# Four more modelled steps in the start-up order of a conv and ELU kernel, with a smaller ScalarE copy, an earlier change of the conv's place and a longer modelled turn

## The chip, the cores and the metric

The kernel runs on one core of one Trainium2 chip. The metric is the device time of one execution in microseconds (us), as the median of several.

## The reference, cut to what matters

```python
# x (8, 4096, 192); weight (8, 7); w_in (192, 2048); w_out (2048, 192)
w = softmax(weight, axis=-1)                 # per head, 7 taps
att = causal depthwise conv of x with w      # 8 heads of 24 channels
h = att.reshape(32768, 192) @ w_in
g = where(h > 0, h, exp(min(h, 0)) - 1)      # ELU
out = g @ w_out
```

Of the kernel before, what the change touches and what calls it, by code (L numbers as in the profile page):

```python
# [34 lines left out]
O_AT = (12, 16)  # L35
CONV_AT = (14, 18, 22, 26)
CONV_POS = ((4, 4), (4, 4), (4, 4), (4, 4))
POS_FROM = 30
QB = 2
WARM = (6, 1, 4)  # L40
WCOLS = ((0, 4 * FC), (4 * FC, 16 * FC))
# [13 lines left out]
HELD = {"h": 2900.0, "c": 1300.0, "a": 1400.0}  # L55

EARLY_CONV = (7, 8, 9, 10)
LATE_Q, COPY_AT = 10, 6
LIVE, UNTIL = 16, 16
EARLY_O = (4, 8)  # L60
LANDS = {"x": {1: 7200.0, 2: 14200.0}, "w_in": 10200.0, "w_out": (3900.0, 8400.0, 11000.0)}
DONE_PE, TO_ACT, TO_POOL, TO_DVE, TO_PE = 165.0, 40.0, 85.0, 35.0, 60.0
ACT_H, ACT_C, ACT_O, POOL_H, DVE_H = 495.0, 470.0, 390.0, 578.0, 600.0
ENDS_ACT, ENDS_POOL, ENDS_DVE, TRANSPOSED = 103.0, 37.0, 84.0, 5000.0
TURNS = 260.0
X_AT = ((2, 1, 1), (1, 1, 0))
ZERO_AT = 8
TAIL = 18
# [2 lines left out]
def bass_lightweight_conv__then__act_elu_kernel(  # L71
# [95 lines left out]
    def o_items(k, g, rt, qs, visit, first, final):  # L167
# [4 lines left out]
        def issue(i):  # L172
# [8 lines left out]
            if ends:  # L181
                visits[k, g] = visit + 1
                turned[k, g] = clock[rt] + MM_O + TURNS

# [147 lines left out]
    for n in range(LIVE, NP):  # L332
# [5 lines left out]
        for m in conv_steps.get(n, []):  # L338
            for rt, later in enumerate(CONV_POS[m % CU] if n >= POS_FROM else (0, 0)):
                later += 3 * rt  # L340
# [770 lines left out]
```

## The kernel before: the parts that the change and the argument touch

The tokens are worked in 32 "supers" of 1024, and each super in 16 blocks of 128 hidden columns: 512 "steps". A step makes two "units", one for each group of 512 tokens. A unit is three H matmuls into one PSUM bank, exp on ScalarE, a clamp on GpSimd, and the ELU join on VectorE, which frees the bank. Sixteen output matmuls a step follow some steps later, and every fourth step has a conv tile, which also takes a bank for a while and is copied out by ScalarE (`csb`). The output accumulators hold two banks and are copied out by ScalarE too (`osb`). Each H or output matmul uses one half of the 128 partitions, so that two can run side by side; the halves are called row groups. The two row groups add to the same accumulator in turns: one waits until the other's visit has ended.

The order of TensorE is fixed when the program is built, by a small planner. It puts each item at a planned time and sorts. Up to step `LIVE` it picks whatever the model says is ready; up to step `UNTIL` it keeps a fixed list for each step but moves its clock on where the model says that something is not ready; after that it only adds up durations:

```python
LATE_Q, COPY_AT = 10, 6      # up to which block ScalarE copies w_in to the upper partitions
LIVE, UNTIL = 16, 16         # live picking, then modelled lists, up to these steps
TURNS = 260.0                # modelled gap between two visits of one accumulator
POS_FROM = 30                # from which step convs go inside the step
CONV_POS = ((4, 4), (4, 4), (4, 4), (4, 4))

def modelled():
    return step[0] < UNTIL

def take_bank(what, rt):                  # the bank that comes free first
    b = min(range(NBANK), key=lambda b: freed[b])
    if modelled():
        clock[rt] = max(clock[rt], freed[b])
    ...

def issue(i):                             # an output matmul
    take_bank(("a", k, g), rt)
    if modelled():
        clock[rt] = max(clock[rt], gt_at[t, g], turned.get((k, g), 0.0) if ... else 0.0)
    ...
for n in range(LIVE, NP):                 # steps after the live part
    ...
    for m in conv_steps.get(n, []):       # convs of super 2: steps 14, 18, 22, 26
        for rt, later in enumerate(CONV_POS[m % CU] if n >= POS_FROM else (0, 0)):
            later += 3 * rt
            lists[rt][later:later] = c_items(m, rt)
```

The upper half of the partitions needs its own copy of w_in. ScalarE and VectorE copy the first blocks, a DMA those from `LATE_Q` on:

```python
if i == COPY_AT:                                        # on ScalarE, after its unit 6
    W(s_w[1], 48)
    upper_half(UPPER[2][0], FC * LATE_Q)
...
c0, c1 = FC * LATE_Q, FF                                # on SyncE
sy.dma_start(w_in[HP:P, :, c0:c1], w_in[0:HP, :, c0:c1]).then_inc(s_wd, 16)
```

## Time and profile before

| What | Value |
|---|---|
| median of the first three runs | 720.21 us (720.03 to 720.96) |
| span of the profiled run | 718.9 us |
| TensorE busy | 99% of the span |
| first H matmul; first VectorE unit | 11.63 us; 14.33 us |
| step 16, 20, 24 (first H matmul) | 31.71, 36.95, 42.37 us |
| four steady steps | 5.44 us |
| last matmul ends | 714.88 us |

The step times are the starts of the first H matmul of a step, found by setting the trace's matmul records beside the program's own order (the counts agree). One more view belongs here, the waits between 31 and 43 us, so steps 16 to 24. It reads "who waited, for whom: us in total, times, longest"; PEld is TensorE's weight load, and in this view a matmul that waits at the head of the queue mostly shows as the wait of its weight load.

```profile
PEld H L1029 <- PE H L1029: 0.9, 4, 0.3
PEld H L1006 <- ACT csb L748: 0.5, 2, 0.3
PEld H L981 <- DVE gT L868: 0.5, 1, 0.5
ACT E L752 <- PE H L1006: 0.4, 1, 0.4
PEld H L1006 <- ACT osb L759: 0.4, 1, 0.4
PEld H L1006 <- DVE gT L868: 0.2, 1, 0.2
```

(Three lines of the view are left out.) The first line is output matmuls that wait for their turn on an accumulator. The second is H tiles whose bank was a conv's, the third the conv of step 18 (L981), which waits for VectorE to free its bank. The fourth is ScalarE, starved by it. The fifth is an H tile (L1006) of step 20, which was given the bank of an output accumulator and waits for ScalarE to copy that out.

### The profile page before, as it was taken

The page shows a single profiled execution, that of the slowest core. Times are in us where ns is not written, and L with a number is a line of the kernel's source. Part 1 is how long each engine was busy: PE and PEld are TensorE (multiplying, and loading weights), DVE is VectorE, ACT ScalarE, POOL GpSimd, SP SyncE. Part 2 cuts the span into 40 slices and gives each one's busy share as a digit, 9 for nine tenths or more (in the row PEclk, how much of TensorE's full clock was granted, in tenths as well). Part 3 has the DMA queues.
Part 4 walks back from the last instruction along what each step waited for, and adds up shares of the span by engine and source line. Part 5 has one row for each costly group of instructions (what it writes and reads, how often), then busy time and mean ns, then how long its engine had stood idle before and what let it go on. Part 6 is the DMA issues. An engine that isn't in the chain of part 4 may idle for free.

```text
span 718.9 us, 27610 instructions
## 1 busy us (share of the span) xinstructions
PE 712.0 (99%) x11847; PEld 683.3 (95%) x11847; DVE 641.5 (89%) x1048; ACT 678.5 (94%) x1289; POOL 664.4 (92%) x1112
## 2 busy tenths in 40 slices
PE   8999999999999999999999999999999999999997
PEld 4699999999999999999999999999999999999997
DVE  7999898998898998899998899988989988999993
ACT  6999999999999999999999999999999999999993
POOL 9989999999999999999999999999999999999893
PEclk9999999999999999999999999999999999999999
DMA  9725434554443553554553344554345544435312
GB/s 178 114 60 83 76 74 75 95 87 70 77 86 72 91 93 63 77 87 80 87 92 67 73 77 94 86 70 86 76 75 96 87 65 79 89 73 84 55 50 68
DMA packets 132303, 58.75 MB, mean 82 GB/s; under 512 B 98374, under 2 KB 131604, under 8 KB 132180
## 3 DMA queue, kind: packets, MB, share of 16 engines
q0 software_dynamic: 43504, 16.77, 22.5%
q1 hardware_dynamic: 88388, 39.32, 22.2%
q8 instruction: 93, 1.52, 0.9%
q10 hardware_dynamic: 288, 0.88, 0.4%
q14 instruction: 30, 0.25, 0.1%
HBM read 34.63 MB, written 25.46 MB: 84 GB/s over the span
## 4 chain that ended last, share of the span: by engine, by line
PE 95%; POOL 2%; DVE 1%; ACT 1%; issue 0%; DVEq 0%; POOLq 0%
PE H L1029 54%; PE H L1006 37%; PE H L981 4%; DVE gT L868 1%; POOL xg L622 1%; ACT E L752 1%; POOL w_in L642 0%; POOL w_out L653 0%; ACT csb L748 0%; POOL E L705 0%; POOL owner L670 0%; ACT osb L759 0%; DVE osb L859 0%; POOL block L680 0%; POOL ident L659 0%
## 5 line engine op out<-in xcount | busy, mean ns | idle before, releaser
L868 DVE SCALAR_TENSOR_TENSOR gT<-E,H 128x512 f16<-128x512 f32 x1024 | 632.0, 683 | 62.2 <-POOL E L705 58.3
L1006 PE MATMUL H<-att,w_in 64*128 64x512 bf16 x3072 | 680.8, 376 | 0.7 <-DVE gT L868 0.5
L1029 PE MATMUL H<-w_out,gT 64*128 64x192 f16 x8192 | 680.7, 243 | 0.1
L705 POOL TENSOR_SCALAR E<-E 128x512 f32<-128x512 f32 x1024 | 603.2, 612 | 41.5 <-ACT E L752 33.9
L1029 PEld LDWEIGHTS H<-w_out,gT 64*128 64x128 f16 x8192 | 608.5, 94 | 16.4 <-PE H L1029 1.6
L752 ACT ACTIVATE E<-H 128x512 f32<-128x512 f32 x1024 | 585.4, 601 | 24.0 <-PE H L1006 1.0
L1006 PEld LDWEIGHTS H<-att,w_in 64*128 64x128 bf16 x3072 | 274.3, 93 | 7.3 <-issue 1.4
L981 PE MATMUL H<-xg,Tm 64*128 64x240 bf16 x496 | 90.9, 263 | 0.2 <-DVE gT L868 0.2
L748 ACT ACTIVATE csb<-H 112x480 bf16<-112x480 f32 x124 | 70.8, 571 | 0.1
L759 ACT ACTIVATE osb<-H 128x384 f32<-128x384 f32 (+1 forms) x129 | 61.9, 482 | 6.9 <-PE H L1029 6.8
L622 POOL DMA_DIRECT2D xg<-in_x_dram x62 | 55.3, 896 | 0.2 <-issue 0.2
L981 PEld LDWEIGHTS H<-xg,Tm 64*128 64x128 bf16 x496 | 42.5, 94 | 1.2 <-DVE gT L868 0.5
L859 DVE COPY osb<-H 128x192 f32<-128x192 f32 x1 | 0.4, 358 | 7.3 <-PE H L1029 7.3
L903 PE MATMUL H<-zw 128*128 128x512 bf16 x10 | 4.0, 548 | 1.2 <-DVE zw L767 1.2
L727 ACT ACTIVATE xb<-xs 128x512 bf16<-128x512 f32 x3 | 1.7, 619 | 2.4 <-DMA xs<-in_x_dram 2.4
L957 PE MATMUL H<-xT,taps 128*128 128x256 bf16 (+1 forms) x24 | 3.9, 317 | 0.0
L903 PEld LDWEIGHTS H<-zw 128*128 128x128 bf16 x10 | 1.1, 125 | 2.8 <-issue 1.4
L957 PEld LDWEIGHTS H<-xT,taps 128*128 128x128 bf16 x24 | 2.2, 97 | 1.5
L642 POOL DMA_DIRECT2D w_in<-in_moe_w_in_dram x6 | 3.6, 610 | 0.0
L653 POOL DMA_DIRECT2D w_out<-in_moe_w_out_dram x3 | 2.5, 869 | 0.0
L720 ACT ACT_TABLE_LOAD x1 | 1.3, 1283 | 1.2 <-PEq L1096 1.2
L733 ACT ACTIVATE w_in<-w_in 64x1536 bf16<-64x1536 bf16 (+1 forms) x2 | 2.3, 1162 | 0.0
(43 smaller groups left out, 19.6 us busy)
## 6 DMA issues: line engine op xcount, KB each, us to landing
out_dram<-osb SPq DMA_DIRECT2D x126, 192.0 KB, 2.8
xg<-in_x_dram POOLq DMA_DIRECT2D x61, 240.0 KB, 4.6
xs<-in_x_dram ACTq DMA_DIRECT2D x1, 768.0 KB, 4.6
w_in<-in_moe_w_in_dram POOLq DMA_DIRECT2D x3, 192.0 KB, 5.4
att<-csb SPq DMA_TRANSPOSE x31, 3.8
w_out<-in_moe_w_out_dram POOLq DMA_DIRECT2D x2, 192.0 KB, 10.1
w_out<-in_moe_w_out_dram POOLq DMA_DIRECT2D x1, 384.0 KB, 13.2
conv_band<-wband SPq DMA_DIRECT2D x1, 288.0 KB, 7.0
```

The lines of the kernel that those rows point to most:

```text
L622: g.dma_start(xg[0:rows, b, 2 * w0 + gr : 2 * w1 : 2, :], src).then_inc(s_x[b][gr], 16)
L642: g.dma_start(w_in[0:HP, j, c0:c1], bass.AP(tensor=moe_w_in.tensor, offset=8 * j * FF + c0, ap=[[CPH * FF, HEADS], [FF, 8], [1, c1 - c0]], ...
L705: g.tensor_scalar(out=E[:, i % NE, :], in0=E[:, i % NE, :], scalar1=1.0, scalar2=0.0, op0=ALU.min, op1=ALU.max,).then_inc(s_clp)
L748: a.activation(*conv_evac(W, m), ACT.Copy).then_inc(s_ce)
L752: a.activation(E[:, i % NE, :], H[:, bank_of[item], :], ACT.Exp).then_inc(s_exp)
L759: a.activation(*out_evac(W, *item[1:]), ACT.Copy).then_inc(s_oev[item[2]])
L868: v.scalar_tensor_tensor(out=gT[:, s % NG3, q, u, :], in0=E[:, i % NE, :], scalar=1.0, in1=H[:, bank_of[item], :], op0=ALU.subtract, op1=A ...
L903: pe.matmul(H[:, bank, :], zw[:, 0:P], zw[:, 0:GS], start=True, stop=True)
L957: ins = pe.matmul(H[:, bank_of[item] + half, c0:c1], taps[:, tap, :], xT[:, j, HALO - PAD + tap + c0 : HALO - PAD + tap + c1], start=(tap ...
L981: ins = pe.matmul(H[:, bank_of["c", m], 256 * q : 256 * q + UC], Tm[rows, h, :], xg[rows, s % NXB, :, CPH * h : CPH * (h + 1)].rearrange(" ...
L1006: ins = pe.matmul(H[:, bank_of[item[:3]], :], w_in[HP * r : HP * (r + 1), j, FC * q : FC * (q + 1)], att[HP * r : HP * (r + 1), s % 2, j, ...
L1029: ins = pe.matmul(acc_of(k, g)[:, D * kb : D * (kb + 1)], gT[HP * rt : HP * (rt + 1), t % NG3, q, g, t0 : t0 + P], w_out[HP * rt : HP * (r ...
```

## The change

It aims at the start: the planner shall know of waits for four more steps, ScalarE shall copy half as much of w_in, the convs of steps 22 and 26 shall stand where those of later steps stand, and the turn of an accumulator shall be planned with more room.

```diff
-POS_FROM = 30
+POS_FROM = 19
...
-LATE_Q, COPY_AT = 10, 6
-LIVE, UNTIL = 16, 16
+LATE_Q, COPY_AT = 9, 6
+LIVE, UNTIL = 16, 20
...
-TURNS = 260.0
+TURNS = 320.0
```

## The prediction

> **What bounds the kernel now.** I read the page first, then two-microsecond and longer windows of the first 60 us, then the chain of waits there, then each engine's timeline there. A "step" below is one of the kernel's 512 blocks of 128 hidden columns for 1024 tokens; it makes two "units" (H tile, exp on ScalarE, clamp on GpSimd, ELU join on VectorE). The page gives 3072 matmuls on L1006 (H), 8192 on L1029 (output) and 496 on L981 (conv), which are exactly the counts of the program, so I could set each record beside the item of the kernel's own order and say which step it belongs to.
>
> ```profile
> span 718.9 us, 27610 instructions
> PE 712.0 (99%) x11847; PEld 683.3 (95%) x11847; DVE 641.5 (89%) x1048; ACT 678.5 (94%) x1289; POOL 664.4 (92%) x1112
> PE 95%; POOL 2%; DVE 1%; ACT 1%; issue 0%; DVEq 0%; POOLq 0%
> ```
>
> TensorE carries the whole span. But its busy share hides lost time early on, so I count matmuls instead (second number of each PE entry, in windows of 6 us):
>
> ```profile
> 14.00:20.00 6.00, 5.42 (x47) 2.58 (x45) 5.67 (x10) 5.95 (x12) 5.91 (x11) 1.00 1.43 236
> 20.00:26.00 6.00, 6.00 (x76) 4.23 (x74) 5.80 (x10) 5.89 (x13) 5.19 (x10) 1.00 1.42 170
> 26.00:32.00 6.00, 6.00 (x65) 3.57 (x62) 5.59 (x11) 5.93 (x13) 5.65 (x11) 1.00 0.43 81
> 32.00:38.00 6.00, 5.71 (x72) 3.65 (x72) 5.88 (x11) 5.61 (x12) 5.66 (x10) 1.00 0.01 3
> 38.00:44.00 6.00, 6.00 (x95) 5.25 (x93) 5.70 (x10) 5.86 (x13) 5.38 (x10) 1.00 0.10 33
> 44.00:50.00 6.00, 6.00 (x107) 5.99 (x103) 5.57 (x10) 5.77 (x12) 5.28 (x9) 1.00 0.43 95
> ```
>
> From 44 us on there are 107 matmuls in 6 us, as later; before it fewer. By start times of first H matmuls, every four steps after step 28 take 5.44 us (1.36 a step) with hardly a deviation to the end: that part is TensorE's own pace. So the end is (moment at which step 24 starts, now 42.37 us) plus a fixed remainder, and only the first 24 steps can give anything. There VectorE is the bound:
>
> ```profile
> 14.33 10.86 DVE L868 SCALAR_TENSOR_TENSOR gT<-E,H 128x512 f16<-128x512 f32 x18 [0.83 <-POOL E L705]
> 25.39 0.69 DVE L868 SCALAR_TENSOR_TENSOR gT<-E,H 128x512 f16<-128x512 f32 x1 [0.20 <-POOL E L705]
> 26.34 1.29 DVE L868 SCALAR_TENSOR_TENSOR gT<-E,H 128x512 f16<-128x512 f32 x2 [0.26 <-POOL E L705]
> 27.78 11.06 DVE L868 SCALAR_TENSOR_TENSOR gT<-E,H 128x512 f16<-128x512 f32 x18 [0.15 <-POOL E L705]
> 39.02 7.57 DVE L868 SCALAR_TENSOR_TENSOR gT<-E,H 128x512 f16<-128x512 f32 x12 [0.18 <-POOL E L705]
> ```
>
> 18 units in 10.86 us is 0.60 us a unit, 1.20 us a step, with three gaps at 25 to 28 us (where four conv tiles pass through ScalarE) and one at 39 us. The reader should see that the gaps are small: little of this stretch is slack.
>
> Where the old order leaves its modelled part, at step 16 (starting 31.71 us), the trace shows what goes wrong:
>
> ```profile
> 33.94 0.38 PE L1006 MATMUL H<-att,w_in 64*128 64x512 bf16 x1
> 34.50 0.27 PE L981 MATMUL H<-xg,Tm 64*128 64x240 bf16 x1 [0.19 <-DVE gT L868]
> 35.28 0.60 ACT L752 ACTIVATE E<-H 128x512 f32<-128x512 f32 x1 [0.39 <-PE H L1006]
> ```
>
> Step 18 begins one H matmul, then the conv of that step stands at the head of the queue and waits 0.56 us after the previous start for its PSUM bank. H of step 18 lies behind it, so ScalarE starves for 0.39 us, and that gap reaches VectorE as 0.12 us at its unit 37 and 0.18 us at unit 39. Two more such waits follow: H of step 19 (36.39 us, its bank is the conv's, released by the csb copy) and H of step 20 (37.86 us, its bank is an output accumulator's, released by the osb copy ending 37.81 us).
>
> **What the Trainium skill says.** PSUM — Partial Sum Buffer, Specifications (TRN2): eight banks of 512 fp32. The trace agrees: an H tile is 128x512 f32, so each unit, conv and accumulator holds a whole bank and the order of bank use matters. TensorE: Matmul & The Clock Gate, The mechanism: matmuls start and end in strict program order. The trace agrees: the H matmuls of step 18 came only with the conv at 34.50 us. VectorE: DVE Perf Modes, Mode 1×: one result a cycle for fp32 and PSUM operands; at its 0.96 GHz 512 columns are 533 ns, the trace's pace is 600 ns. ScalarE: Activation LUTs, What ACT_TABLE_LOAD costs: 186 ns + 0.833 ns a column, so 768 columns estimate to 826 ns; the trace's copy took 842 ns.
>
> **The change part by part.**
> (1) Steps 16 to 19 get the early model: there the planner now moves its clock on when a bank, an ELU result or an accumulator turn is not ready, and sorts other work ahead. The amount of work is unchanged. Value: through step 17 the trace follows the plan at a constant distance (12.15 us at H of step 17); at step 24 the distance is 13.65 us. So 1.5 us are lost against a TensorE-only ideal in steps 18 to 24, 0.56 at the conv, 0.3 in step 19, 0.4 at H of step 20, the rest in 21 to 24. But VectorE caps the gain: from its unit 36 (36.75 us) to unit 48 (44.71 us) it takes 7.96 us, and twelve units at 0.60 are 7.20 us, so 0.76 us is available without leaning on the queue in front of it. Counted from step 16 to 24 as a whole the cap is 10.66 − 8×1.20 = 1.06 us. Steps 20 to 23 stay unmodelled, and their waits of about 0.4 us will partly remain. Of 0.76 I expect some three quarters: −0.6 us.
> (2) One block fewer copied by ScalarE: 768 columns become 384 (three column groups of 128 instead of 256), an estimate of 384×0.833 = 0.32 us less on ScalarE at 16.3 us. Beside what? GpSimd waited only 0.09 us for the unit after it and VectorE not at all (its first 18 units have no gap), and by the H tile of step 7 ScalarE was waiting for TensorE again. So the saving is hidden: 0 to −0.1 us. Its counterpart: step 9's second H now needs the DMA copy, 336 KB instead of 288. That landed at 20.71 us, an estimate of 7/6 of its 6.7 us gives 21.8 us; the H is issued at 22.94 us. No wait.
> (3) Conv's place from step 19 on: the convs of steps 22 and 26 go behind four output matmuls, as in all later steps. From step 24 to 28 the old place takes 5.45 us, the new place 5.44 later on: 0.01 us. In step 22 it may lift a conv off the head of the queue: 0 to −0.1 us.
> (4) The turn of an accumulator is modelled as 320 instead of 260 ns. It adds no instruction; it moves the second half of a pair of output matmuls back in the early order, where VectorE is bound and TensorE has room: ±0.1 us.
> Sum: −0.6 −0.05 −0.05 = −0.7 us on a median of 720.21, so 719.5 us.
>
> **The rivals.** (a) *VectorE takes it all*: the order gets better but VectorE at 0.60 us a unit was the bound anyway. For it: four gaps only, 0.3 us of them after step 16. Then the gain is 0.2 us or less: 720.0. (b) *The waits only move*: the unmodelled part now starts at step 20, where output work doubles and accumulators change hands, so the bank waits of steps 18 to 20 reappear at 20 to 23; or the banks fall differently for the rest of the run. Against it: once TensorE is the bound (step 24) its waits vanish whatever the phase, and convs in the new place are what all later steps have. Time 720.1 to 720.7. (c) *A full recovery*: VectorE runs unbroken, the queue before it is used too, 1.0 to 1.2 us: 719.1. (d) *The DMA copy comes late* and blocks step 9, TensorE's strict order making everything wait: 0.5 to 1 us slower. Against it: more than 1 us of slack by the estimate above.
>
> **Range and chances.** Weights about 25% for (a), 15% for (b), 20% for (c), 3% for (d), the rest on the sum; the three runs of before spread over 0.9 us, so the range is 718.8 to 720.4. Two per cent would be 14.4 us, while all that the first 24 steps lose to order is about 1.5 us: within 2% is nearly certain.
>
> **What would show it.** In the profile after: step 18's conv without a wait ahead of it, no ScalarE gap near 35 us, VectorE unbroken from 27.8 us to about 42 us, step 24 starting some 0.7 us sooner (41.7 instead of 42.37 us), more matmuls than 72 and 95 in the windows 32:38 and 38:44, still 107 afterwards, and 5.44 us for four steps as before. The gaps of VectorE at 25 to 28 us should stay. I would be wrong if step 24 starts no sooner, if these early gaps are what moves, if the second H of step 9 waits for the DMA, or if four steady steps take other than 5.44 us.

## More of the kernel before

All runs named "fast" are of the chip's undisturbed state.

The later rounds ran on other chips of the machine (the records name chips 0, 2 and 5), so totals are compared only within their own rounds.

## The result, and the profile after

The changed kernel took 720.26 us (median of six runs, 719.74 to 720.73), the kernel before 720.33 us in the same rounds (720.03 to 720.96). The ratio of 0.9998 (95% interval 0.9985 to 1.001) is the mean time of one kernel's fast runs over that of the other's of the same rounds, so it is not quite the ratio of the two medians. By itself it does not tell a gain of 0.7 us from none.

The trace tells more. This is the page of the changed kernel, its head and the summary of the chain that ended last:

```profile
span 718.6 us, 27608 instructions
PE 97%; POOL 2%; DVE 0%; ACT 0%; issue 0%; DVEq 0%; POOLq 0%
```

TensorE's share of the chain rose from 95% to 97%: in the first 45 us the chain now runs over TensorE where it ran over VectorE and ScalarE before. The chain is inferred, and it does not say that VectorE has room there: dve30 below shows that it has hardly any. The windows of 6 us, to be set beside those in the prediction (the second number of a pair counts instructions, the first pair is TensorE):

```profile
26.00:32.00 6.00, 6.00 (x66) 3.17 (x61) 5.70 (x11) 5.93 (x13) 5.67 (x11) 1.00 0.42 79
32.00:38.00 6.00, 6.00 (x78) 3.87 (x74) 6.00 (x12) 5.87 (x13) 5.67 (x10) 1.00 0.01 3
38.00:44.00 6.00, 6.00 (x98) 5.31 (x95) 5.75 (x11) 5.87 (x13) 5.52 (x10) 1.00 0.10 33
44.00:50.00 6.00, 6.00 (x106) 5.97 (x103) 5.58 (x10) 5.82 (x12) 5.37 (x10) 1.00 0.49 109
```

From 32 to 38 us there are 78 matmuls instead of 72, from 38 to 44 us 98 instead of 95, and then the same pace as before. VectorE's timeline (start, duration, count, and the gap before with its releaser):

```profile
14.30 10.27 DVE L868 SCALAR_TENSOR_TENSOR gT<-E,H 128x512 f16<-128x512 f32 x17 [1.03 <-POOL E L705]
24.87 2.72 DVE L868 SCALAR_TENSOR_TENSOR gT<-E,H 128x512 f16<-128x512 f32 x4 [0.31 <-POOL E L705]
27.74 19.73 DVE L868 SCALAR_TENSOR_TENSOR gT<-E,H 128x512 f16<-128x512 f32 x32 [0.15 <-POOL E L705]
```

The break at 39.02 us is no longer worth a row of its own, though a gap of 0.14 us is left at the same unit, the 39th counted from 0. The early gaps moved by one unit but add up to the same, 0.61 us. And here is step 18 on TensorE and the ScalarE rows at that time, from the two timelines:

```profile
33.73 0.96 PE L1006 MATMUL H<-att,w_in 64*128 64x512 bf16 x4
34.47 0.38 PE L981 MATMUL H<-xg,Tm 64*128 64x240 bf16 x2
```

```profile
33.66 1.66 ACT L752 ACTIVATE E<-H 128x512 f32<-128x512 f32 x3
35.31 0.57 ACT L748 ACTIVATE csb<-H 112x480 bf16<-112x480 f32 x1
36.01 1.15 ACT L752 ACTIVATE E<-H 128x512 f32<-128x512 f32 x2
```

The three H matmuls of step 18's first tile are now issued before the conv (before, one of them was), so ScalarE's idle time of 0.39 us before its unit 36 is gone, and one of 0.13 us (35.88 to 36.01) before unit 37 is left. But the conv itself starts at 34.47 us, as late as before (34.50). The waits from 31 to 43 us:

```profile
PEld H L1029 <- PE H L1029: 0.5, 3, 0.2
PEld H L1006 <- DVE gT L868: 0.4, 2, 0.2
PEld H L1029 <- DVE gT L868: 0.3, 1, 0.3
PEld H L981 <- DVE gT L868: 0.3, 1, 0.3
PEld H L1006 <- ACT csb L748: 0.2, 1, 0.2
```

The waits of TensorE for the `osb` copy and of ScalarE for TensorE are gone from this list. In their place stand waits for VectorE (gT), at other items. The waits for an accumulator's turn fell from 0.9 to 0.5 us; from 45 to 57 us the view shows none in either kernel.

In numbers: counted from the first VectorE unit, which removes the jitter of the first loads, step 16 comes at 17.38 us in both kernels, step 20 at 22.57 instead of 22.63 us, and step 24 at 27.69 instead of 28.04 us. From step 24 to the last matmul it is 672.51 and 672.52 us. So the change gains 0.35 us, nearly all in steps 20 to 24, and in this pair of traces keeps it to the last matmul. That last stretch scatters, though: two more traces of the changed kernel (again, again2) show 672.59 and 672.69 us, so that at the last matmul the gain is only resolved as 0.2 to 0.35 us.

### The profile page after: what moved, and what is told of

Same layout as the page of the kernel before. It is cut to its first block, busy times and chain, and to the rows that moved or that the text cites. A ratio compares the mean times of both kernels' runs of the same rounds, so it can differ in the third digit from the quotient of the medians.

```text
span 718.6 us, 27608 instructions
## 1 busy us (share of the span) xinstructions
PE 712.1 (99%) x11846; PEld 682.6 (95%) x11847; DVE 641.3 (89%) x1048; ACT 678.2 (94%) x1289; POOL 664.2 (92%) x1112
## 4 chain that ended last, share of the span: by engine, by line
PE 97%; POOL 2%; DVE 0%; ACT 0%; issue 0%; DVEq 0%; POOLq 0%
PE H L1029 55%; PE H L1006 38%; PE H L981 4%; POOL xg L622 1%; POOL w_in L642 0%; POOL w_out L653 0%; DVE gT L868 0%; POOL E L705 0%; ACT E L752 0%; POOL owner L670 0%; ACT csb L748 0%; DVE osb L859 0%; POOL block L680 0%; POOL ident L659 0%; POOL ones L657 0%
```

## The experiments

The mark that I use is "step 24": the start of its first H matmul, counted from the start of the first VectorE unit. The kernels with the same TensorE order as another repeat it within 0.01 us, so it resolves what the total cannot.

| Kernel | step 16 | step 20 | step 24 | VectorE unit 48 |
|---|---|---|---|---|
| before | 17.38 | 22.63 | 28.04 | 30.38 |
| changed | 17.38 | 22.57 | 27.69 | 30.09 |
| again, again2 (changed) | 17.38, 17.37 | 22.57, 22.56 | 27.69, 27.69 | 30.10, 30.09 |
| u20 | 17.38 | 22.57 | 27.82 | 30.16 |
| pos19 | 17.39 | 22.63 | 28.00 | 30.46 |
| t320 | 17.41 | 22.65 | 28.06 | 30.40 |
| late9 | 17.39 | 22.62 | 28.04 | 30.38 |
| u20p19 | 17.40 | 22.59 | 27.72 | 30.11 |
| u24 | 17.37 | 22.35 | 27.69 | 30.09 |
| dve30 | 17.38 | 23.05 | 28.17 | 30.58 |
| act30 | 17.38 | 22.92 | 28.05 | 30.45 |
| shortact | 17.37 | 22.56 | 27.62 | 29.83 |
| dve100 | 17.38 | 22.56 | 27.69 | 30.09 |

### Which part gives the 0.35 us: u20, pos19, t320, late9, u20p19

**u20**: four more modelled steps alone.

```diff
-LIVE, UNTIL = 16, 16
+LIVE, UNTIL = 16, 20
```

> The kernel before with UNTIL 20 alone (four more modelled steps; convs, turns and copy as before). I measure from the first VectorE unit to the first H matmul of step 24: 28.04 us before, 27.69 changed. Theory A (the modelled steps give the gain): 27.7, and the 5.41 us of steps 20 to 24 become about 5.1. Rival (conv's place in step 22 gives it): 28.0 and 5.4. Steps 16 to 20 lose the ScalarE gap at 35 us in both.

Step 24 came at 27.82 us, so this part alone gives 0.22 us. ScalarE's idle time near 35 us is down to 0.14 us (before unit 37), nearly as in the changed kernel. Steps 20 to 24 take 5.25 us (27.82 − 22.57), between the two theories. VectorE's timeline runs on as one row here too:

```profile
27.80 19.86 DVE L868 SCALAR_TENSOR_TENSOR gT<-E,H 128x512 f16<-128x512 f32 x32 [0.15 <-POOL E L705]
```

**pos19**: the conv's place alone.

```diff
-POS_FROM = 30
+POS_FROM = 19
```

> The kernel before with POS_FROM 19 alone (conv of steps 22 and 26 behind four output matmuls). Theory A: first VectorE unit to step 24 stays at 28.0 us, or gains under 0.1. Rival: most of the 0.35 us, so 27.7. The conv wait of step 18 at 34.5 us must stay in both, as step 18 is not touched.

Step 24 at 28.00 us: 0.04 us, as theory A has it. VectorE is even later at unit 48 (30.46 us), as the gap before its unit 45 grew to 0.24 us. The conv of step 18 waits as before, as expected (it starts 20.18 us after the first VectorE unit in both). The rival falls.

**t320**: the turn alone.

```diff
-TURNS = 260.0
+TURNS = 320.0
```

> The kernel before with TURNS 320 alone (early order only). Theory A: VectorE is the bound there, so the first VectorE unit to step 16 stays 17.38 us within 0.1 and to step 24 28.0 us. Rival (the turns free TensorE's queue early): step 16 earlier by 0.1 to 0.2 us and that kept to step 24.

Step 16 at 17.41 and step 24 at 28.06 us: nothing gained, 0.02 to 0.03 us lost. It is this part that moves the early VectorE gap from unit 18 to unit 17 (0.31 us there), without a change of their sum. The rival falls.

**late9**: the smaller ScalarE copy alone.

```diff
-LATE_Q, COPY_AT = 10, 6
+LATE_Q, COPY_AT = 9, 6
```

> The kernel before with LATE_Q 9 alone: the order of TensorE is the same as before, only ScalarE's copy shrinks from 768 to 384 columns (842 ns to an estimated 520 ns) and the DMA copy grows to 336 KB. Theory A: hidden, the first 18 VectorE units stay without a gap and step 24 stays at 28.0 us after the first unit; the DMA lands before 22 us. Rival (ScalarE is the bound of the start): 0.3 us sooner.

Step 24 stays at 28.04 us. This is the ScalarE copy and then VectorE's first units:

```profile
16.71 0.52 ACT L733 ACTIVATE w_in<-w_in 64x384 bf16<-64x384 bf16 x1
```

```profile
14.49 10.86 DVE L868 SCALAR_TENSOR_TENSOR gT<-E,H 128x512 f16<-128x512 f32 x18 [1.12 <-POOL E L705]
```

The copy fell from 0.84 to 0.52 us (the formula in the Trainium skill, ScalarE: Activation LUTs, What ACT_TABLE_LOAD costs, estimates 506 ns for 384 columns), and VectorE still takes 18 units in 10.86 us without a gap, to the hundredth as before. The saving is hidden. This run alone would be a weak test, because in it ScalarE happened to begin its unit 6 0.27 us later after the first VectorE unit than in the kernel before. The changed kernel adds to it: its unit 7 on ScalarE, just behind the shorter copy, begins 0.24 us sooner (2.58 instead of 2.82 us), and by unit 14 nothing of that is left (6.38 us in both). The DMA copy landed at 21.72 us, before the H matmul that needs it, and no wait for it shows.

**u20p19**: the first two together.

```diff
-POS_FROM = 30
+POS_FROM = 19
-LIVE, UNTIL = 16, 16
+LIVE, UNTIL = 16, 20
```

> The kernel before with UNTIL 20 and POS_FROM 19 together. Alone they moved the distance from the first VectorE unit to step 24 from 28.04 us to 27.82 and 28.00; the whole change reaches 27.69. If the conv's place pays only once the four steps are modelled, 27.7 (turns and copy add nothing); if the two simply add, 27.78, and the turns or the copy give the rest.

Step 24 at 27.72 us. So on top of the modelled steps the conv's place is worth 0.10 us, against 0.04 alone: the parts do not quite add. Turns and copy together give the last 0.03 us, little more than the repeat of the mark.

### Is the gain real in the total: again, again2

Both are the changed kernel, five rounds each.

> The changed kernel once more, five rounds. The profiles say that its last matmul ends 0.38 us sooner than before's. If that is real and the spread of single runs (about 0.9 us) hides it, the ratio over more runs is 0.9995 (720.0 against 720.3); theory that something after the matmuls gives it back: 1.000. The markers inside the trace repeat within 0.1 us.

> The changed kernel, five more rounds. From the traces the last matmul ends 0.35 us sooner, and the time after it varies by about 1 us from run to run with either kernel. Ratio between 0.9985 and 1.0005, centre 0.9995.

The first gave 720.46 us against 721.2 us, a ratio of 0.9986 (0.9974 to 0.9999). The second gave 720.58 against 721.0 us, a ratio of 0.9996 (0.9982 to 1.0009). With the first result (0.9998) the three ratios average 0.9993, which is 0.5 us; the trace's 0.35 us would be a ratio of 0.9995, which lies in all three intervals. The marks repeat (table above). What hides most of the gain in the profiles is the end: from the last matmul to the end of the span the profiles of all kernels show 3.24 us (pos19) to 4.31 us (dve30), with no relation to the change. The last stores are issued by SyncE, and these issues vary; the row of pos19, then that of dve30:

```profile
713.05 3.27 SPq L557 DMA_DIRECT2D out_dram<-osb  x5
```

```profile
713.10 4.42 SPq L557 DMA_DIRECT2D out_dram<-osb  x5
```

The same five issues take 3.27 us in one run and 4.42 us in another. They are not the whole of it: in `again` they take 3.33 us, yet its end is 4.22 us long, and there the store that ScalarE issues lands last, 3.2 us after its issue (2.2 us in the kernel before). Why they vary is not shown.

### Why only 0.35 us: u24, dve30, act30, shortact, dve100

**u24**: modelled up to step 24, five rounds.

```diff
-LIVE, UNTIL = 16, 20
+LIVE, UNTIL = 16, 24
```

> The changed kernel with UNTIL 24: the four steps with doubled output work are modelled too. Theory A (the waits of unmodelled steps 20 to 23 remain, about 0.2 us of VectorE gaps): step 24 sooner by 0.1 to 0.2 us than in the changed kernel (27.5 us after the first VectorE unit). Rival (VectorE and its five-bank ring are the bound, order can give no more): 27.7, no change. Total between 719.8 and 720.3.

Step 20 begins 0.22 us sooner than in the changed kernel (22.35 us), and step 24 not at all (27.69 us). Total 720.36 us, just outside the range that I gave; before took 721.2 us in the same rounds, and the ratio is 0.9988 (0.9975 to 1.0002). VectorE's gaps at units 39 and 45 stay at 0.14 and 0.11 us. So modelling steps 20 to 23 too wins nothing at step 24; theory A as I put it falls.

**dve30**: a memset of 512 columns on VectorE before its unit 30.

```diff
+                if i == 30:
+                    v.memset(part[:, 0, :], 0.0)
                 W(s_clp, i + 1)
                 v.scalar_tensor_tensor(
```

> The changed kernel with one extra VectorE memset of 512 fp32 columns (some 0.3 to 0.6 us) just before its unit 30. If VectorE is the cap in these steps, step 24 comes later by nearly the whole duration of the memset; if TensorE's order or ScalarE is, by little or nothing.

```profile
33.33 0.48 DVE L868 MEMSET part<- 128x512 f32 x1
33.73 14.28 DVE L870 SCALAR_TENSOR_TENSOR gT<-E,H 128x512 f16<-128x512 f32 x23
```

The unit behind it starts 0.55 us later than in the changed kernel, from the first unit on (19.37 instead of 18.83 us). Step 20 comes 0.48 us later, and step 24 too (28.17 us). Of a delay on VectorE at unit 30, 0.48 of 0.55 us go through to step 24: up to step 20 VectorE has less than 0.1 us of room.

**act30**: a copy of 512 columns on ScalarE before its unit 30.

```diff
+                    if i == 30:
+                        a.activation(xb[:, 0, :, :], xs[:, 0:XI, 0:HP], ACT.Copy)
                     a.activation(
                         E[:, i % NE, :], H[:, bank_of[item], :], ACT.Exp
```

> The changed kernel with one extra ScalarE copy of 512 fp32 columns (some 0.5 us of issue) before its unit 30. If ScalarE is the cap, step 24 comes later by about 0.5 us; if VectorE alone is, the queue on GpSimd and VectorE (about 0.6 us ahead there) swallows most of it and step 24 moves by 0.2 us or less.

The copy took 0.62 us. ScalarE's unit 30 starts 0.43 us later, VectorE shows a gap of 0.27 us at that unit, and step 24 comes 0.36 us later (28.05 us). That is neither of the two values expected: the queue ahead of VectorE holds about 0.1 us (0.43 − 0.36), not 0.6. The trace of the changed kernel says so too: from the start of a unit on ScalarE to its start on VectorE it takes 1.39 us at unit 30, against 1.32 us at best (unit 45); only by unit 36 has it grown to 1.98 us. ScalarE is not the bound, but it is within 0.1 us of being it.

**shortact**: wrong (relative error 0.125). ScalarE copies only half of the columns of the convs of steps 18 and 22, and of the first two accumulators; the other halves are zeroed in the start-up, which delays all by some 2 us and does not touch the marks.

(The lines that zero the other halves are left out.)

```diff
-                    a.activation(*conv_evac(W, m), ACT.Copy).then_inc(s_ce)
+                    to, at = conv_evac(W, m)
+                    if m in (9, 10):
+                        to, at = to[:, 0:1], at[:, 0:1]
+                    a.activation(to, at, ACT.Copy).then_inc(s_ce)
...
-                    a.activation(*out_evac(W, *item[1:]), ACT.Copy).then_inc(s_oev[item[2]])
+                    to, at = out_evac(W, *item[1:])
+                    if item[1] == 0:
+                        to, at = to[:, 0:D], at[:, 0:D]
+                    a.activation(to, at, ACT.Copy).then_inc(s_oev[item[2]])
```

> The changed kernel with wrong results on purpose: ScalarE copies only half of the columns of the convs of steps 18 and 22 and of the first two output accumulators (the other halves are zeroed at the start). It saves ScalarE some 0.2 + 0.2 + 0.16 + 0.16 us between units 36 and 48, and touches no order. If ScalarE's copies make the VectorE gaps that remain (units 39 and 45), these gaps shrink and step 24 comes 0.2 to 0.4 us sooner (27.3 to 27.5 us after the first unit); if VectorE and the banks alone are the cap, 27.7.

VectorE's timeline between 30 and 46 us, first of the changed kernel, then of this one:

```profile
29.54 16.73 DVE L868 SCALAR_TENSOR_TENSOR gT<-E,H 128x512 f16<-128x512 f32 x27
```

```profile
29.78 16.47 DVE L877 SCALAR_TENSOR_TENSOR gT<-E,H 128x512 f16<-128x512 f32 x27
```

The 27 units take 0.26 us less; the gap at unit 39 is gone (0.14 us before), that at unit 45 halved (0.11 to 0.05 us). So ScalarE's copies make the gaps that remained. But step 24 came only 0.07 us sooner (27.62 us), well short of the 0.2 to 0.4 us expected. VectorE is ahead by 0.26 us, and TensorE uses only 0.07 us of it: in steps 20 to 24 VectorE is no longer the main thing that holds TensorE. (The shorter copies also free the banks of the convs and accumulators sooner, so this run does not test VectorE alone.)

**dve100**: the memset of dve30, but at unit 100.

```diff
+                if i == 100:
+                    v.memset(part[:, 0, :], 0.0)
```

> The control for the earlier run with a VectorE memset at unit 30 (step 24 came 0.48 us later): the same memset at unit 100, in step 50. If TensorE is the bound from step 24 on, the time from step 24 to the last matmul stays 672.5 us within 0.15; if VectorE is near its bound there too, 673.0.

From step 24 to the last matmul 672.69 us. The same kernel without the memset shows 672.51, 672.59 and 672.69 us, so this mark is too coarse for the 0.15 us that I had set. The step marks settle it: step 56, six steps behind the memset, comes within 0.01 us of where it comes in again and again2. Nothing is lost: once TensorE is the bound, VectorE has room for it.

No version tried beats the changed kernel: u24 is equal to it.

## Why the prediction was right or wrong

The measured median of 720.26 us lies in the range of 718.8 to 720.4, and within 2% was right. The range holds the kernel before too (720.33 us in the same rounds), so lying in it shows no gain. The point of 719.5 us was too hopeful by about half of the gain: the traces show 0.35 us, not 0.7.

- **What bounds the kernel: right.** The remainder after step 24 is 672.5 us in both kernels, and only the first 24 steps gave anything. dve100 shows that VectorE has room after step 24, and dve30 that up to step 20 it has next to none. What the prediction left out is ScalarE, which act30 finds within 0.1 us of being the bound as well. Its count of VectorE's gaps after step 16 (0.3 us) also misses one of 0.12 us at unit 45, which the timeline view did not break a row for.
- **(2), the ScalarE copy: right.** The copy fell by 0.32 us as worked out, and late9 shows all of it hidden. The DMA copy held up nothing.
- **(3), conv's place: right in size.** 0.04 us alone, 0.10 us with the modelled steps, which is the edge of what was given.
- **(4), the turn: right in size.** 0.02 us lost alone.
- **(1), "Of 0.76 I expect some three quarters: −0.6 us": the mis-sized term.** The modelled steps give 0.22 us alone, and 0.35 us with everything. The mechanism was the right one: ScalarE's gap at 35 us shrank, the waits for the csb and osb copies in front of steps 19 and 20 went or shrank; u20 alone shows the same. The cap was wrong. I took VectorE's pace of 0.60 us a unit for the bound up to step 24, and TensorE as able to follow. VectorE went from unit 36 to 48 in 7.68 us (36.71 to 44.39 us) instead of 7.96, so 0.28 of the 0.76 us. The rest, 0.48 us, is mostly in two places where its starts lie 0.8 instead of 0.6 us apart, at units 39 and 45, and shortact, with four of ScalarE's copies halved, wins 0.26 us of it. But it shows also that winning it back on VectorE is worth just 0.07 us at step 24.
- The likely reason, argued and not tested, lies in the work of steps 20 to 23. There the second half of the first super's output begins, and each step has 12 output matmuls instead of 8. From the steady 5.44 us for four steps, less the 16 output matmuls that these four have fewer at 82 ns apart and two at a time (0.66 us), TensorE's own work there is an estimate of 4.78 us; VectorE's is eight units at 0.60, so 4.80 us for four steps. ScalarE's is close too, an estimate of 4.7 us: eight units at 0.48 us, the closest that they start behind one another, one conv copy (0.47) and one accumulator copy (0.37). The three bounds meet just there, with six banks or fewer between them, and each waits for another now and then. Measured were 5.41 us before and 5.12 us after. I counted a cap by one engine where three were about equally near.
- **"Step 18's conv without a wait ahead of it": wrong.** It waits as before (34.47 us, its row group idle for 0.52 us in both kernels), as VectorE frees its bank only then (its unit 31 ends at 34.41 us). I had listed 0.56 us there as loss of order. The new order leaves this wait; what it removes is that the H matmuls of step 18's first tile stand behind it. Whether another place of this conv would spare the wait is not shown: with POS_FROM at 19, no run moves it.
- **The other signs.** The windows came as said (78 and 98 matmuls, then 106) and four steady steps take 5.44 us. ScalarE's gap near 35 us shrank to 0.13 us and is not gone, VectorE keeps a gap of 0.14 us at unit 39, and step 24 starts at 41.99 us, not 41.7. One of the early gaps moved, which was named as a sign of being wrong; it moved by one unit without a change of their sum.
- **Rivals.** (a), VectorE takes it all, fits steps 16 to 20, where only 0.06 us was gained (u24 has step 20 itself 0.22 us sooner, and VectorE no further at unit 48: 30.09 us in both). (b), the waits only move, holds in part: the waits for osb went and waits for VectorE came at other items of steps 20 and 21, and u24, which models those too, gains nothing. (c) and (d) fell.

What stays open is how the 0.3 us divides that steps 20 to 24 still take above either engine's own pace. shortact puts 0.07 us of it to ScalarE's copies; the rest I could argue (too few banks) and did not test, as there is no ninth bank to give. The waits for an accumulator's turn are a rival that no run isolates: in the changed kernel H of steps 21 and 24 starts 0.12 and 0.13 us late behind an output matmul that waits for its turn. Against it speaks u24, which shows 0.3 us of such waits instead of 0.5 and starts step 24 no sooner.

## What to carry to other kernels

When a start-up goes from one bound to another, work out the pace of every engine over the same steps before taking the slowest one's gaps as the possible gain; where they are nearly equal, as here, removing a wait mostly uncovers another. A wait at the head of an in-order queue has two costs, its own and that of what stands behind it, and here the better order removed only the second. Marks inside the trace, counted from an early event, resolve a gain of 0.05 us where the total scatters by a whole microsecond.

## What the Trainium skill lacked or had wrong

- TensorE: Matmul & The Clock Gate, The mechanism, says that matmuls keep program order in start and end. The start records here do not quite: in the kernel before, 2537 of its 11760 H, output and conv matmuls (matched in order within each line) start before one that stands ahead of them in the program, all but one of them in the other row group, by 0.06 us in the median and 0.30 us at most. So the prediction's "the trace agrees" holds only as far as the wait of step 18 goes.
- The same section does not tell what a wait at the head of the queue costs with two row groups: a conv of one row group that waited for its bank also stopped the H matmuls of the other, whose bank was ready (row group idle for 0.36 us at 34.52 us before; in the changed order the H is done by then).
- No page that I read tells how much the issue of a few stores at the end varies on SyncE: the same five took 3.27 us in one run and 4.42 us in another, and the span after the last matmul varied from 3.24 to 4.31 us.
